# Second half of batch 0 as three one-pass products instead of four-pass ones, with a newly ordered step list

## The chip, the cores and the metric

The kernel runs on one core of one Trainium2 chip. The metric is the device time of one execution in microseconds (us), lower is better. In the profile the engines are PE (matrix multiply), PEld (its weight loads, which overlap the multiplies), DVE (vector), ACT (scalar), POOL (GpSimd) and SP (which issues most of the transfers).

## What is computed

Two blocks follow each other. The first is a chunked linear scan with decay (4 batches, 8 heads, 768 positions, head size 32, state size 16). The second is a mixer on its output, laid out as 4 batches of 768 positions by 256 channels. The weights reach the kernel as 64-bit floats.

```python
for c in range(nc):                                  # the scan, chunk by chunk
    cum = np.cumsum(la, axis=-1)
    M = CB * L                                       # L = exp(cum_i - cum_j), causal
    y[:, :, sl] = einsum(M, xc) + einsum(Cc, state) * exp(cum)
    state = decay_full * state + sum(Bx)
...
h = xt @ U @ V                                       # the mixer, rank 32 over positions
u = x + h.transpose(0, 2, 1)
ch = np.maximum(u @ w_ch1, 0.0) @ w_ch2              # 256 -> 1024 -> 256 channels
return (u + ch)
```

## The kernel before

**The order is written out by hand.** The string `PLAN` is a list of words; `follow` takes them one after another, and each word calls one small function that issues its instructions to the queues of the engines. Each engine works through its own queue strictly in that order. Nothing is scheduled by a compiler, so the position of a word in the list decides what stands ahead of it on every engine that it uses. Two more strings, `BANKS` and `SLOTS`, hold one letter or digit for each allocation, in the order of the list: `BANKS` says which of the 8 banks of the accumulator memory a result goes to, `SLOTS` which of 15 buffers (a to o, tile `words`) a piece of weights or of hidden values takes.

**The scan.** A batch is 768 positions in three pairs of 128-position blocks, so there are twelve pairs, k = 0 to 11. For each of them the words `P T g m M s u i n j y t` scale, transpose, form the products and their causal mask, carry the state, and copy the result out (`yT`, and by `t` the transposed `ytok`). `B` and `X` load its inputs, `E` issues PE fillers that keep the array busy.

**The mixer of a batch b.** `p`, `q` and `a` make `u = x + h` in place in `yT`. Each batch is cut into two halves of 384 positions, j = 0 and 1. Then come the two large products, in one of two ways:

- *plain* (line 813, word `U b.j.m`): full 32-bit products, which the array does in four passes. For one of the 8 groups m of 128 hidden channels, two matmuls of 128x384 read `w1f` (the first weights) and `yT`; ACT writes `relu` into `gT`. The second product (word `d b.j.k.n`, line 845) then takes 4 pieces n of two four-pass matmuls of 128x256.
- *in three parts*: word `S` (line 795) splits `u` into a rounded part, a remainder and a combination; ACT makes the first, DVE the other two. Word `f` (line 821) issues 6 one-pass matmuls of 128x384; ACT writes the rounded `relu`, and word `h` (line 831) has DVE write the remainder, and for every odd m also the combination of a pair (`joined`). The second product then takes 6 pieces of four one-pass matmuls of 128x256. The results carry the factor 1/`MORE`, which `summed` and the scale of `pT` (line 752) take out again.

Before the change, batch 0 is done plainly in both halves (`PLAIN = 2`, and `parts = b or j >= PLAIN` in `down`), batches 1 to 3 in three parts. The last piece of each `d` adds one more matmul, the sum on DVE (`ytok`) and the store.

**The weights.** Words `w` load pieces of the 64-bit weights. Word `c` turns a piece into 32-bit floats in three steps: two DVE operations and one on ACT, then one on DVE, then one on POOL. Word `R` makes the three parts of a piece, in two steps for the first weights (`R0` to `R3`: ACT; then POOL, ACT and DVE) and three for the second (`R4` to `R7`, DVE only in the third). The first weights in plain form (`w1f`) lie in the same buffer as the split `u` (tag "u", one buffer, lines 241 and 798). So the first `S` of the kernel can't write before the last `U` and the last `R0` to `R3` have read.

In all of it DVE's calls go through one helper at line 180, so its rows all carry that line; PE's mixer products all carry line 805.

Of the kernel before, what the change touches and what calls it, by code (L numbers as in the profile page):

```python
# [12 lines left out]
UINT32 = mybir.dt.uint32  # L13
FP32R = mybir.dt.float32r
WCOLS = 512
PLAIN = 2
BANKS = (
    '0120020340056712340512304672360475123605473605127463207546132076547654762054726013725472543176'
    '0176430253025301725301725164512513047640726134526130574062642026420135720457204132204620137374'
    '105743741065247346531057215231523175412376270376065262141645')  # L20
SLOTS = (
    'abcdefghijklmnocabidfejcgahfimjohimdfjohmlbkeongaecnifmknidjkbolhgacenjfidkmolbhcfgajkendgcloj'
    'amihbegadonfkmlbcf')


NEAR = 1.0 - 2.0 ** -13
# [1 line left out]
MORE = (1.0 + EPS) ** 2  # L28
LESS = 1.0 / (1.0 + EPS)
AF = mybir.ActivationFunctionType  # L30
ALU = mybir.AluOpType
# [7 lines left out]


PLAN = (
# [32 lines left out]


@with_exitstack
def kernel(
# [27 lines left out]
    nc = tc.nc  # L105
# [63 lines left out]
    class Kept:  # L169
# [15 lines left out]
    vector = Kept(nc.vector)  # L185
# [7 lines left out]
        out=a_sb,  # L193
# [46 lines left out]
    w1 = [const.tile([P, NCB, DF], FP32R, name=f"w1{i}") for i in range(3)]  # L240
# [487 lines left out]
    def mixer(b):  # L728
# [4 lines left out]
        def project():  # L733

            p = bank("w", DM)
            if b < 2:
                for c in range(NC):
                    nc.tensor.matmul(out=p[ts(c % 4, Q)], lhsT=U_sb[:, c], rhs=ytok[b][:, c],  # L738
                                     start=c < 4, stop=True, skip_group_check=True)
            else:  # L740
                seen = set()
                for c in range(0, NC, 2):
                    for half in range(NCB):
                        for v in range(2):
                            to = (c + 2 * half) % 4 + v
                            nc.tensor.matmul(out=p[ts(to, Q), ts(half, P)], lhsT=U_sb[:, c + v],  # L746
                                             rhs=ytok[b][:, c + v, ts(half, P)],
                                             start=to not in seen, stop=True, skip_group_check=True)
                            seen.add(to)
            hold["p"] = pT = mix.tile([P, DM], FP32, tag="pT", name="pT", bufs=1)  # L750
            if b:
                nc.scalar.activation(pT, p, AF.Copy, scale=1.0 / MORE)
            else:
                nc.scalar.copy(out=pT, in_=p)

        def parted():

# [18 lines left out]

        def summed(to, t, u):

            if b:
                return vector.scalar_tensor_tensor(out=to, in0=t, scalar=MORE, in1=u,  # L780
                                                   op0=ALU.mult, op1=ALU.add)
            return vector.tensor_tensor(out=to, in0=t, in1=u, op=ALU.add)

        def halves(near, far, both, v):

# [27 lines left out]
        def plain(j, m):  # L813

            if (j, m // 2) not in gT:
                gT[j, m // 2] = pair(FP32)
            t = bank("xz"[m % 2], HS)
            products(t, [(w1f[m // 2][:, n, ts(m % 2, P)], block(n, j)) for n in range(NCB)], True)
            nc.scalar.activation(gT[j, m // 2][:, m % 2], t, AF.Relu)

        def up(j, m):

# [165 lines left out]
```

## Time and profile before

| | us |
|---|---|
| time, median of 3 runs (lowest, highest) | 225.58 (222.82, 225.99) |
| time of the profiled execution | 226.02 |
| its span, first to last instruction | 224.3 |
| PE busy | 214.9 (96%) |
| DVE busy | 144.9 (65%) |
| ACT busy | 86.7 (39%) |
| POOL busy | 35.3 (16%) |

Busy time is an average over stages that differ. The first stage, up to about 36 us, is the scan of batch 0 with the first transfers; from there to about 70 us the plain products of batch 0 run beside the conversion of the weights and the scan of batch 1; the rest is batches 1 to 3. A row of the profile names the tile that is written, the tile read, the shapes, the count, the busy time and the mean of one in ns.

### The profile page before, as it was taken

The page shows a single profiled execution, that of the slowest core. Times are in us where ns is not written, and L with a number is a line of the kernel's source. Part 1 is how long each engine was busy: PE and PEld are TensorE (multiplying, and loading weights), DVE is VectorE, ACT ScalarE, POOL GpSimd, SP SyncE. Part 2 cuts the span into 40 slices and gives each one's busy share as a digit, 9 for nine tenths or more (in the row PEclk, how much of TensorE's full clock was granted, in tenths as well). Part 3 has the DMA queues.
Part 4 walks back from the last instruction along what each step waited for, and adds up shares of the span by engine and source line. Part 5 has one row for each costly group of instructions (what it writes and reads, how often), then busy time and mean ns, then how long its engine had stood idle before and what let it go on. Part 6 is the DMA issues. An engine that isn't in the chain of part 4 may idle for free.

```text
span 224.3 us, 6923 instructions
## 1 busy us (share of the span) xinstructions
PE 214.9 (96%) x3012; PEld 185.1 (83%) x3012; DVE 144.9 (65%) x300; ACT 86.7 (39%) x195; POOL 35.3 (16%) x49
## 2 busy tenths in 40 slices
PE   7888999999799999999999999999999999999994
PEld 4656655676466888998999999999999999999993
DVE  4697559587975882167693857757645955944651
ACT  2443742675486541143466022344623232232100
POOL 3012220526461390200000010200000000000000
PEclk9985799999999999999999999999999999999998
DMA  5988777888395500002144200100000000001012
GB/s 78 140 149 99 163 144 102 223 220 109 101 133 79 116 25 23 23 3 75 12 67 64 73 3 23 35 17 6 1 3 0 23 26 25 0 23 50 0 47 94
DMA packets 69662, 14.56 MB, mean 65 GB/s; under 512 B 63808, under 2 KB 67840, under 8 KB 69632
## 3 DMA queue, kind: packets, MB, share of 16 engines
q1 hardware_dynamic: 69488, 14.06, 32.1%
q8 instruction: 23, 0.38, 0.7%
q14 instruction: 7, 0.06, 0.1%
q10 hardware_dynamic: 144, 0.07, 0.1%
HBM read 10.98 MB, written 3.15 MB: 63 GB/s over the span
## 4 chain that ended last, share of the span: by engine, by line
PE 72%; DVE 2%; DVEq 0%; issue 0%
PE x L805 36%; PE z L805 25%; PE y L685 2%; PE w L712 2%; PE y L649 1%; PE x L535 1%; PE w L495 1%; DVE words L180 1%; PE w L569 1%; DVE w L180 1%; PE w L759 1%; PE w L746 1%; PE z L769 0%; PE x L769 0%; PE w L738 0%; PE z L535 0%
## 5 line engine op out<-in xcount | busy, mean ns | idle before, releaser
L180 DVE SCALAR_TENSOR_TENSOR words<-words 128x768 fp32r<-128x768 f32 (+3 forms) x35 | 29.3, 838 | 1.9 <-PE x L805 0.4
L805 PE MATMUL x<-w2c,words 128*128 128x256 f32 x160 | 30.1, 321 | 0.0
L805 PE MATMUL x<-u,w 128*128 128x384 f32 x144 | 29.9, 343 | 0.0
L805 PE MATMUL z<-u,w 128*128 128x384 f32 x144 | 29.2, 341 | 0.0
L805 PE MATMUL x<-w,words 128*128 128x256 f32 x192 | 29.1, 286 | 0.0
L829 ACT ACTIVATE words<-x 128x384 fp32r<-128x384 f32 x24 | 11.7, 491 | 37.8 <-PE x L805 37.7
L805 PEld LDWEIGHTS x<-w2c,words 128*128 128x128 f32 x160 | 24.9, 189 | 1.5
L805 PEld LDWEIGHTS x<-w,words 128*128 128x128 f32 x192 | 25.8, 190 | 0.1
L805 PEld LDWEIGHTS x<-u,w 128*128 128x128 f32 x144 | 24.6, 188 | 0.6 <-DVE u L180 0.3
L805 PEld LDWEIGHTS z<-u,w 128*128 128x128 f32 x144 | 24.8, 188 | 0.4 <-issue 0.2
L829 ACT ACTIVATE words<-z 128x384 fp32r<-128x384 f32 x24 | 11.8, 492 | 25.1 <-PE z L805 25.1
L180 DVE SCALAR_TENSOR_TENSOR words<-x,words 128x384 fp32r<-128x384 f32 x24 | 13.2, 552 | 10.6 <-ACT words L829 8.0
L180 DVE SCALAR_TENSOR_TENSOR words<-z,words 128x384 fp32r<-128x384 f32 x24 | 13.2, 550 | 5.8 <-ACT words L829 5.8
L180 DVE SCALAR_TENSOR_TENSOR S<-S,kept,w 128x64 f32<-128x64 f32 x40 | 11.2, 280 | 6.8 <-PE w L569 5.1
L805 PE MATMUL z<-w2c,words 128*128 128x256 f32 x80 | 15.3, 323 | 0.0
L685 PE MATMUL y<-M,x 64*32 64x64 f32 x768 | 13.1, 234 | 2.2 <-DVE M L180 1.8
L805 PE MATMUL z<-w,words 128*128 128x256 f32 x96 | 15.0, 285 | 0.0
L685 PEld LDWEIGHTS y<-M,x 64*32 64x32 f32 x768 | 9.2, 112 | 6.6 <-issue 2.5
L596 POOL TENSOR_TENSOR Sm<-S,own 128x256 f32<-128x256 f32 (+1 forms) x12 | 7.8, 650 | 36.1 <-DVE S L180 36.1
L805 PEld LDWEIGHTS z<-w,words 128*128 128x128 f32 x96 | 13.2, 189 | 0.1
L805 PEld LDWEIGHTS z<-w2c,words 128*128 128x128 f32 x80 | 12.5, 189 | 0.7
L535 PE MATMUL x<-Cm,T 32*64 32x128 f32 x192 | 11.4, 317 | 1.2 <-ACT Cm L505 0.7
(142 smaller groups left out, 356.1 us busy)
## 6 DMA issues: line engine op xcount, KB each, us to landing
words<-in_moe_w_ch_dram SPq DMA_DIRECT2D x7, 512.0 KB, 5.8
x<-in_x_dram SPq DMA_DIRECT2D x24, 128.0 KB, 3.4
out_dram<-ytok SPq DMA_DIRECT2D x23, 128.0 KB, 1.7
bc<-in_B_dram SPq DMA_DIRECT2D x24, 64.0 KB, 3.0
bc<-in_C_dram SPq DMA_DIRECT2D x12, 128.0 KB, 3.3
words<-in_moe_w_ch_dram SPq DMA_DIRECT2D x2, 256.0 KB, 5.1
words<-in_moe_U_dram SPq DMA_DIRECT2D x1, 192.0 KB, 3.2
words<-in_moe_V_dram SPq DMA_DIRECT2D x4, 48.0 KB, 2.1
```

The costliest lines, as they stand in the source:

```text
L180: self.last = call(*args, **kwargs)
L495: nc.tensor.transpose(out=tp[:, i, v], in_=s["BC"][:, i, c + v].rearrange("p h n -> p (h n)"), identity=ident)
L535: nc.tensor.matmul(out=s["g"][r][cols, c], lhsT=s["T"][rows, 0, c, cols], rhs=s["Cm"][rows, :, :, ts(2 * c + p, Q)].rearrange("r v t i -> ...
L569: nc.tensor.matmul(out=s["A"][p][ts(r, Q), v], lhsT=s["BC"][half, 0, v, 2 * r:2 * r + 2].rearrange("p h n -> p (h n)"), rhs=x_sb[k][half, ...
L596: nc.gpsimd.tensor_tensor(out=s["Sm"][:, sl], in0=s["S"][:, sl].rearrange("p i (s d) -> p i s d", s=2), in1=own2[:, b, 4 * q + sl.start:4 ...
L649: nc.tensor.matmul(out=channels(k)[r // 2][ts(r % 2, H), c, p], lhsT=own[ts(r, Q)], rhs=st[k]["T"][ts(r, Q), 1, :, ts(2 * c + p, Q)].rearr ...
L685: product = nc.tensor.matmul(out=y[n][ts(i, Q), c, p], lhsT=x_sb[k][half, c, h], rhs=s["M"][half, h // 2, c, h % 2], start=fresh(k, n, [i] ...
L712: nc.tensor.transpose(out=t[:, c, g], in_=yT[b][:, g, ts(2 * q + c, P)], identity=ident)
L746: nc.tensor.matmul(out=p[ts(to, Q), ts(half, P)], lhsT=U_sb[:, c + v], rhs=ytok[b][:, c + v, ts(half, P)], start=to not in seen, stop=True ...
L759: nc.tensor.matmul(out=p, lhsT=spot.rearrange("p q r -> p (q r)"), rhs=hold["p"], start=True, stop=True, skip_group_check=True)
L805: nc.tensor.matmul(out=t, lhsT=lhsT, rhs=rhs, start=start, stop=True, skip_group_check=True)
L829: nc.scalar.activation(gs[j, m // 2][0][:, m % 2], t, AF.Relu, scale=NEAR)
```

## The change

`PLAIN` becomes 1. Half j = 0 of batch 0 is still done plainly, half j = 1 in three parts. In the list the 8 words `U0.1.m` go; `S0.1`, 8 words `f0.1.m`, 8 words `h0.1.m` and two more pieces for each of the three `d0.1.k` come in. Since both halves of a batch share `pT`, `ps` and `u`, batch 0 now carries the factor 1/`MORE` throughout: the conditions on `b` go, and the plain `relu` is scaled by it too. The last `U` of the plain half and all of `R0` to `R3` now stand ahead of `S0.1`.

The list, the banks (248 to 249 letters) and the slots (112 to 120) are new throughout; the multiset of all other words is the same but for the fillers (`E1` three times before; `E2`, then `E1` three times). Quoted of the list is the stretch from the first up product to the second split of batch 1.

```diff
-PLAIN = 2
+PLAIN = 1
...
-    'E1 E1 A0 YB0 YB1 Q1.0 Q0.0 Q0.1 YX0 A1 Q0.2 Q1.2 K0 YB2 YU0 YV0 V0.0.0 E1 V0.1.1 V1.0.2 s0 YX1 '
...
-    'T4 c1 X5 w3 w4 g3 j2 c2 m3 c2 y2 T4 c2 M3 O2.1 p0 c1 g4 m4 q0 n3 M4 s3 a0.0 a0.1 c1 c3 U0.0.1 '
-    'U0.1.1 c3 U0.0.0 j3 c3 P5 s4 w5 u3 R0 R1 T5 U0.0.3 u4 T5 P6 U0.1.0 i3 g5 w7 y3 i4 M5 c4 n4 s5 '
-    'B10 X6 m5 c4 c5 c5 c4 U0.0.2 t3 T6 T6 U0.1.3 U0.1.2 B7 j4 n5 c6 y4 w6 c5 u5 g6 M6 i5 R1 R2 '
-    'U0.1.5 c6 c8 U0.0.6 m6 B9 c8 s6 j5 y5 n6 X7 U0.0.4 R3 U0.1.6 P7 T7 T7 R0 X8 c6 t5 t4 c7 c8 '
-    'U0.1.7 R3 U0.0.7 U0.0.5 c7 R2 B8 U0.1.4 p1 u6 w8 s7 X9 R4 j6 u7 g7 m7 i6 q1 P8 c7 c9 P10 '
...
+    'E2 YX0 A1 YB0 A0 Q0.0 Q0.2 YB1 Q0.1 K0 YX1 Q1.0 YB2 V0.0.0 YB3 YX2 V0.1.1 s0 E1 u0 g0 E1 B4 '
...
+    'y0 V2.1.3 n1 P3 g2 m2 P4 w1 s2 O0.0 M2 T3 T4 c0 u2 T3 i1 T4 j1 i2 c1 y1 g3 c1 n2 E1 j2 C0 y2 '
+    'C0 s3 m3 C0 t1 c0 c0 u3 w2 O2.1 v0 p0 M3 c4 c4 g4 c2 c2 q0 c2 n3 w4 c4 i3 m4 B5 a0.0 X4 c3 R2 '
+    'c3 a0.1 U0.0.1 c1 R2 R0 c3 R1 M4 X5 B6 U0.0.4 U0.0.0 U0.0.5 P5 c5 w6 U0.0.3 T5 T5 s4 j3 c5 R0 '
+    'y3 B8 c5 U0.0.2 u4 g5 R3 w5 i4 M5 X6 U0.0.6 B7 m5 n4 P6 n5 s5 R1 R3 w8 u5 c7 U0.0.7 j4 j5 S0.1 '
+    'c7 i5 y4 y5 T6 T6 P8 t3 c7 t4 t5 c6 c6 f0.1.2 f0.1.0 p1 c6 g6 h0.1.2 h0.1.0 R4 w7 M6 m6 s6 u6 '
+    'P7 f0.1.6 d0.0.0.0 f0.1.4 X8 R4 f0.1.3 c9 B11 d0.0.2.0 h0.1.6 c8 f0.1.1 q1 d0.0.1.0 d0.0.0.1 '
+    'c8 c9 d0.0.1.1 c8 h0.1.4 h0.1.3 d0.0.2.1 f0.1.7 c9 B9 R6 a1.0 d0.0.1.2 R5 h0.1.7 f0.1.5 R7 '
+    'd0.0.2.2 X7 d0.0.1.3 d0.1.2.0 R5 a1.1 d0.1.1.0 S1.0 d0.1.1.1 R6 T7 T7 d0.0.2.3 R7 P9 d0.0.0.2 '
+    'R4 T8 d0.1.2.1 d0.1.0.0 R5 f1.0.2 h0.1.1 R6 d0.1.0.1 h0.1.5 f1.0.4 d0.0.0.3 f1.0.5 d0.1.2.2 '
+    'B10 f1.0.6 d0.1.0.2 T8 d0.1.2.3 d0.1.0.3 h1.0.4 h1.0.2 R7 d0.1.1.2 h1.0.6 d0.1.2.4 d0.1.0.4 n6 '
+    'h1.0.5 s7 u7 f1.0.0 d0.1.2.5 d0.1.1.3 h1.0.0 d0.1.0.5 g7 i6 m7 j6 s8 f1.0.3 u8 y6 M7 d0.1.1.4 '
+    'd0.1.1.5 g8 h1.0.3 X9 i8 f1.0.7 f1.0.1 m8 M8 n8 X11 n7 i7 j8 s9 h1.0.7 j7 S1.1 h1.0.1 y8 T9 y7 '
...
@@ project
-            if b:
-                nc.scalar.activation(pT, p, AF.Copy, scale=1.0 / MORE)
-            else:
-                nc.scalar.copy(out=pT, in_=p)
+            nc.scalar.activation(pT, p, AF.Copy, scale=1.0 / MORE)
@@ summed
-            if b:
-                return vector.scalar_tensor_tensor(out=to, in0=t, scalar=MORE, in1=u,
-                                                   op0=ALU.mult, op1=ALU.add)
-            return vector.tensor_tensor(out=to, in0=t, in1=u, op=ALU.add)
+            return vector.scalar_tensor_tensor(out=to, in0=t, scalar=MORE, in1=u,
+                                               op0=ALU.mult, op1=ALU.add)
@@ plain
-            nc.scalar.activation(gT[j, m // 2][:, m % 2], t, AF.Relu)
+            nc.scalar.activation(gT[j, m // 2][:, m % 2], t, AF.Relu, scale=1.0 / MORE)
```

More of the change, by code (lines that the diff above doesn't have):

```diff
@@ L15 @@
 WCOLS = 512
-PLAIN = 2
+PLAIN = 1
 BANKS = (
-    '0120020340056712340512304672360475123605473605127463207546132076547654762054726013725472543176'
-    '0176430253025301725301725164512513047640726134526130574062642026420135720457204132204620137374'
-    '105743741065247346531057215231523175412376270376065262141645')
+    '0120203456700123445670142536742536017535607135442716047213560472013202135602136504726513715304'
+    '2671532041567320315310210167547645045301454130762541302764512643026423034104321506415730673241'
+    '0673410614564250164015735713713742746346101250615602734032473')
 SLOTS = (
-    'abcdefghijklmnocabidfejcgahfimjohimdfjohmlbkeongaecnifmknidjkbolhgacenjfidkmolbhcfgajkendgcloj'
-    'amihbegadonfkmlbcf')
+    'abcdefghijklmnofadichbemgkjodhbfmgimlhamegmengkmebjkcfdoclighmaonebckjfgldiombhekfacjgndileokm'
+    'ajghfbcodinlmekhancfgbjldi')
 NEAR = 1.0 - 2.0 ** -13
```

46 rows, old and new, of the table PLAN are left out of this document.

## The prediction

> **What bounds the kernel now.** I read the page first, then engine use by stretches, then PE's waits, the chain of waits, and the mean of each group of DVE instructions.
>
> ```profile
> span 224.3 us, 6923 instructions
> ```
>
> The profiled execution took 226.02 us: this span and 1.7 us around it. It lies 0.4 above the median of the three runs, 225.58, so 0.4 comes off any sum made against it.
>
> ```profile
> 10.00:15.00 5.00, 3.77 (x103) 2.18 (x103) 3.85 (x15) 2.54 (x10) 0.79 (x2) 0.98 0.87 152
> 15.00:25.00 10.00, 9.44 (x281) 6.58 (x281) 6.55 (x22) 4.82 (x16) 1.47 (x4) 0.50 0.87 137
> 36.00:70.00 34.00, 32.23 (x525) 20.89 (x528) 26.85 (x52) 21.26 (x47) 15.21 (x13) 1.00 0.72 142
> 55.00:60.00 5.00, 3.47 (x75) 2.00 (x75) 4.75 (x7) 3.27 (x7) 2.88 (x3) 1.00 0.35 112
> 70.00:221.00 151.00, 151.00 (x1790) 143.32 (x1782) 93.93 (x171) 49.65 (x104) 12.49 (x14) 1.00 0.13 32
> ```
>
> Columns: stretch, its length, then the busy time of PE, PEld, DVE, ACT and POOL, the granted clock, the DMA share and GB/s. From 70 us to the end PE never rests: what is taken from PE there comes off the time. From 36 to 70 us PE rests 1.8 us in 34, DVE is busy 79%. At 55 to 60 us the two change places: PE is at 3.47 of 5, DVE at 4.75. Before 25 us PE runs ten microseconds at half clock.
>
> The DVE timeline shows what made PE rest at 58 to 60 us, and the waits of PE name it:
>
> ```profile
> 57.61 1.84 DVE L180 TENSOR_SCALAR words<-words 128x512 f32<-128x512 f32 x2
> 59.37 0.74 DVE L180 TENSOR_TENSOR M<-x,causal 128x256 int32<-128x256 int32 x2
> ```
>
> ```profile
> PE y L685 <- DVE M L180: 1.5, 1, 1.5
> ```
>
> The opening of a `c` (two operations, 1.84) stood ahead of a mask, and PE waited 1.5 us for the mask. So batch 0 lives off two engines: its plain products need nothing of DVE, and DVE uses that time to prepare weights and scan. The change takes work from PE and puts work on DVE exactly there.
>
> **The change part by part.** PE first. The chain of waits gives what a piece takes where PE runs without a gap:
>
> ```profile
> 64.70 3.87 PE z L805 x12
> ...
> 73.44 1.73 PE x L805 x8
> ...
> 168.45 0.47 PE z L805 x4
> 168.93 1.05 PE x L805 x6
> ```
>
> A four-pass matmul leaves two records. The first row is three `U` (six matmuls): 1.29 us each. The second is two four-pass pieces of `d`: 0.865 each. The third is one piece of `d` in one-pass form, 0.47, and the last one `f`, 1.05. Eight `U` become eight `f`: 8 x (1.29 - 1.05) = 1.9 us less. Twelve pieces of `d0.1` become eighteen: 12 x 0.865 - 18 x 0.47 = 1.9 us less. PE loses 3.8 us of work, all of it later than the first up product.
>
> DVE's means, costliest first:
>
> ```profile
> L180 DVE SCALAR_TENSOR_TENSOR words<-words 128x768 fp32r<-128x768 f32 x24 | 23.0, 959 | 1.8 <-PE x L805 0.4
> L180 DVE SCALAR_TENSOR_TENSOR words<-z,words 128x384 fp32r<-128x384 f32 x24 | 13.2, 550 | 5.8 <-ACT words L829 5.8
> ...
> L180 DVE SCALAR_TENSOR_TENSOR S<-S,kept,w 128x64 f32<-128x64 f32 x40 | 11.2, 280 | 6.8 <-PE w L569 5.1
> L180 DVE TENSOR_TENSOR M<-x,causal 128x256 int32<-128x256 int32 x24 | 9.0, 418 | 5.1 <-PE z L535 5.0
> ...
> L180 DVE SCALAR_TENSOR_TENSOR u<-yT,u 128x768 fp32r<-128x768 f32 x6 | 6.8, 1130 | 0.0
> L180 DVE TENSOR_TENSOR u<-yT,u 128x768 fp32r<-128x768 f32 x6 | 6.6, 1107 | 2.8 <-ACT u L800 2.8
> L180 DVE TENSOR_TENSOR BC<-bc,F 128x512 f32<-128x512 f32 x9 | 6.3, 697 | 0.0
> L180 DVE TENSOR_SCALAR words<-words 128x512 int32<-128x512 int32 x7 | 6.2, 889 | 0.0
> L180 DVE SCALAR_TENSOR_TENSOR w<-words,w 128x512 fp32r<-128x512 f32 x4 | 5.9, 1486 | 1.4 <-POOL words L452 1.4
> L180 DVE SCALAR_TENSOR_TENSOR words<-words 128x512 int32<-128x512 int32 x7 | 4.8, 683 | 0.1
> L180 DVE SCALAR_TENSOR_TENSOR ytok<-x,ytok 128x256 f32<-128x256 f32 x11 | 4.7, 424 | 9.2 <-PE x L805 9.1
> L180 DVE SCALAR_TENSOR_TENSOR yT<-x,yT 128x384 f32<-128x384 f32 x6 | 3.3, 554 | 2.7 <-PE x L769 2.6
> ...
> L180 DVE TENSOR_SCALAR words<-words 128x512 f32<-128x512 f32 x7 | 2.9, 419 | 0.0
> L180 DVE TENSOR_TENSOR words<-w,w 128x512 f32<-128x512 f32 x4 | 2.7, 684 | 0.0
> ```
>
> DVE gains `S0.1` (1.11 + 1.13), eight `h` at 0.55 and four joins at 0.96: 2.24 + 4.4 + 3.84 = 10.5 us. ACT gains the first part of the split:
>
> ```profile
> L800 ACT ACTIVATE u<-yT 128x768 fp32r<-128x768 f32 x6 | 5.0, 841 | 3.5 <-DVE yT L180 3.5
> ```
>
> It is 0.84 us on an engine with 13 us free between 36 and 70 us; nothing. The new factor costs nothing: the sums change their form, not their size (the row `ytok`, 0.42, is that form already), and ACT scales in the pass that it makes anyway.
>
> How fast does DVE work such a list off? Two of its rows mark the ends of a run in the present list, the last sum of `a0.1` and the last state step of `u6`:
>
> ```profile
> 36.91 0.55 DVE L180 TENSOR_TENSOR yT<-z,yT 128x384 f32<-128x384 f32 x1
> ...
> 68.08 0.92 DVE L180 SCALAR_TENSOR_TENSOR S<-S,kept,w 128x64 f32<-128x64 f32 x3
> ```
>
> Between 37.5 and 69.0, 31.5 us, the list has six openings of `c` (0.42 + 0.89), six second steps (0.68), three `P` (0.70), four masks of two (0.84), 15 state steps (0.28) and four `R` (1.49): 7.9 + 4.1 + 2.1 + 3.4 + 4.2 + 6.0 = 27.7 us by the means. That is 0.88 of list work in each microsecond, with some of the rest waits for PE.
>
> First cut in the new list, from the first up product to `f0.1.2`. DVE up to the end of the split: four `R`, three masks, two `P`, two openings and one second step of `c`, seven state steps, the split: 6.0 + 2.5 + 1.4 + 2.6 + 0.7 + 2.0 + 2.2 = 17.4 us. PE has eight `U` (10.3) and 15 steps of the scan. Their price comes from this row of the same stretch, line 805 alone (PE, PEld):
>
> ```profile
> 36.00:70.00 34.00, 22.35 (x64) 11.52 (x64) 1.00 0.72 142
> ```
>
> 32.23 - 22.35 = 9.9 us for about 20 such steps of scan, 0.49 each (a pair of `T` as one); 15 make 7.4. PE: 17.7 us. At full pace DVE is ready, at 0.88 it needs 19.8 and PE waits 2.1. The chain at the split itself (`U0.0.7` must have read the buffer, then ACT 0.84, DVE 2.24: 3.1 us) lies under seven scan steps, `j4` to `t5`, 3.4 us; without them it would cost 3.1 in full. I take 1.0 for this wait, half way.
>
> Second cut, from the split on to `S1.1`, which `f1.1.7` needs. DVE: three openings and four second steps of `c`, three `P`, 15 `h` and seven joins, six masks, 11 state steps, the four sums of `a1`, six of `d0`, four last steps of `R`, two splits: 3.9 + 2.7 + 2.1 + 15.0 + 5.0 + 3.1 + 2.2 + 2.5 + 2.7 + 4.5 = 43.7 us. PE: 16 `f` (16.8), twelve four-pass pieces (10.4), 20 one-pass pieces (9.4) and 21 scan steps (10.3): 46.9 us before `p1`, `q1` and `a1` are counted. Over both cuts it is DVE 61.1 against PE 64.6: the first cut decides as long as DVE holds more than 0.92, and at 0.88 (69.4) the wait grows to 4.8.
>
> Ahead of the first up product DVE gets two more steps of `c4`, one of `c3` and `u3`, and loses `M4`: about 2.0 + 0.7 + 1.1 - 0.8 = 3.0 us more, against one more scan step on PE (0.5). Its cover is DVE's idle time there, 3.45 us from 15 to 25 us and 1.15 from 10 to 15. So 0 to 2.5; I take 0.7, nearer the covered end. The third filler `E1` stands where PE waits anyway.
>
> SP's queue: `X0` now goes out ahead of `B0`, by this row 1.6 us of issue:
>
> ```profile
> 5.43 1.57 SPq L208 DMA_DIRECT2D x<-in_x_dram  x2
> ```
>
> The first scaling may start later by up to 1.6, and `s0`, which needs `X0`, earlier by as much; I take 0. `w3` moves ahead of `w1` and all of the first weights come sooner; the DMA share is 0.72 to 0.87 there, so they fit.
>
> Sum against 226.0: PE -3.8; the old wait for the mask goes with the order that made it, -1.5 (0 if a like one comes instead); the wait at the split +1.0 (0 to 4.8); the start +0.7 (0 to 2.5). That gives 222.4; less 0.4 for the median, about 222.
>
> **The rivals.** *The half clock goes.* PE is at half clock from 15 to 25 us, and two of the new fillers stand just before. At full clock the stretch's PE work would take 4.7 us; DVE needs 6.55, so at most 3.45 is gained: 219 and, with no wait at the split, 217. For it: one run of three of the same kernel took 222.82, 3.2 less than the profiled one. Against it: nothing says that a filler of a few tenths decides. The longest wait that PE itself shows from 8 to 36 us is this:
>
> ```profile
> PE x L535 <- ACT Cm L505: 0.7, 1, 0.7
> ```
>
> [...]
>
> *DVE becomes the bound (slower).* Place: from the first up product to `S1.1`. If DVE works its 61.1 us of list off at 0.79 of the time, which is its busy share from 36 to 70 us, it needs 77.3 and PE waits 12.7 in all: 226.0 - 3.8 + 12.7 = 234.9, or 234.5 on the median. The point from which it shows as slower by 2% is a wait of 8.3, a pace of 0.84. For it: `h` waits for ACT, which waits for PE, so DVE's list is now full of steps that can't be done ahead; and accumulator banks stay taken until `h` has read them. Against it: 0.88 was reached while DVE waited for PE.
>
> **How the numbers follow.** The forecast, most of the saving left, has 0.46; its own range is 220 (no wait) to 226.5 (4.8, old wait replaced). The clock going has 0.26, at 217 to 221. DVE as the bound has 0.28, at 228 to 235, of which 0.02 lies inside 2%. Two per cent, about what a measurement of this kernel can tell from no change, is 221.1 and 230.1. Faster: 0.26 and 0.07 of the forecast's low end, 0.33. Slower: 0.26. Within: 0.41. The range 217.5 to 232 leaves out the end of the clock case and the upper half of the slow one.
>
> **What would show it.** Rows for `f0.1` at 1.05 for six and `d0.1` at 0.47 for four; 56 thirds instead of 48 and 28 joins instead of 24. PE should show a wait on DVE's `u` of about 1 us near 56 us, and be dense from there. The half clock shows in the granted clock. If PE waits over 5 us for DVE's `words`, `u` or M between 55 and 105 us, DVE was the bound; if PE is dense from 40 us on, the forecast is too high.

## The result, and the profile after

| us | before | after |
|---|---|---|
| median (lowest, highest), 20 runs each, same chip | 225.20 (222.82, 227.25) | 222.36 (221.63, 224.09) |
| time of the profiled execution, its span | 226.02, 224.3 | 223.10, 221.4 |
| start of the first up product, in the profile | 36.21 | 37.44 |
| start of the last matmul, in the profile | 220.77 | 217.81 |
| the stretch between these two | 184.56 | 180.37 |

The ratio of the times is 0.9904, 95% interval [0.9876, 0.9932]. The stretch became 4.19 us shorter, and it began 1.23 us later: 2.96 us, as the spans say (2.9). All experiments below are read by these two marks, the first row of line 801 (805 before) and the last. Some runs of each kernel fall into a slower state, which the medians contain and the ratios leave out.

The page after, its busy times and the granted clock in 40 slices:

```profile
span 221.4 us, 7025 instructions
...
PE 210.0 (95%) x3054; PEld 186.6 (84%) x3054; DVE 151.7 (69%) x314; ACT 87.2 (39%) x196; POOL 35.8 (16%) x47
...
PEclk9995699999999999999999999999999999999999
...
PE 74%; DVE 10%; DMA 4%; SPq 4%; issue 2%; POOL 2%; ACT 2%; POOLq 0%; DVEq 0%
```

PE lost 4.9 us of busy time and DVE gained 6.8. The slices at 5 and 6 tenths show that the half clock has stayed. The last line is the chain that ended last; its shares can't be set beside those of before (PE 72%, DVE 2%), because that chain could be followed back only to 55 us. Its pieces say more: from 53.3 to 77.2 us it runs over DVE, ACT and POOL without a piece of PE, and from there nearly all of it is PE. So there is now a stretch in which DVE, not PE, carries the end:

```profile
71.52 2.04 DVE words L181
73.56 0.93 DVE yT L181 x2
...
74.99 1.85 DVE words L181
...
77.23 1.22 PE z L801 x8
```

The changed kernel in the stretches of the prediction (length, then PE, PEld, DVE, ACT, POOL, granted clock, DMA share, GB/s), and PE's waits from 36 us to the end:

```profile
15.00:25.00 10.00, 8.12 (x168) 5.52 (x168) 7.39 (x23) 4.10 (x11) 1.13 (x2) 0.56 0.85 150
...
36.00:70.00 34.00, 33.00 (x504) 24.89 (x504) 30.12 (x59) 21.58 (x47) 16.76 (x15) 1.00 0.78 149
55.00:60.00 5.00, 5.00 (x69) 4.15 (x68) 4.97 (x8) 4.70 (x11) 1.77 (x2) 1.00 0.86 129
70.00:218.00 148.00, 146.91 (x1828) 141.62 (x1826) 97.31 (x176) 49.08 (x103) 11.71 (x12) 1.00 0.14 32
```

```profile
PE y L686 <- POOL settled L609: 0.6, 1, 0.6
PE y L650 <- issue: 0.6, 1, 0.6
PE z L801 <- DVE ytok L181: 0.5, 1, 0.5
PE z L801 <- DVE yT L181: 0.4, 1, 0.4
```

The wait of 1.5 us for a mask is gone, and at 55 to 60 us PE is full where it was at 3.47 of 5. There is no wait for `u`: the split ended at 56.01 and `f0.1.2` began at 56.23, straight behind the transposes before it. In exchange PE, which was without a gap behind 70 us, now waits twice there: 0.5 us at 77.2 for a sum of DVE, 0.6 at 153.5 for POOL's `settled`. The third wait, "issue", is one for which the profile names nothing; the last section comes back to it.

What a product and a piece take on PE, where they follow each other (start, duration, line, operation):

```profile
81.74 1.22 PE L801 MATMUL x<-u,w 128*128 128x384 f32 x6
82.80 0.64 PE L801 MATMUL x<-w,words 128*128 128x256 f32 x4
83.27 1.04 PE L801 MATMUL x<-u,w 128*128 128x384 f32 x5
```

From start to start `f` takes 1.06 us and the one-pass piece of four matmuls 0.47, as taken. So a matmul called four-pass (1.29 for the two of a `U`, 0.865 for the two of a piece, two records each) took 3.6 to 3.7 times one called one-pass; that the array makes four passes for it isn't shown by any row, the word is only a name here.

DVE's groups by form, and its timeline where PE waits for the sum (a row with x2 holds two instructions):

```profile
L181 DVE SCALAR_TENSOR_TENSOR words<-words 128x768 fp32r<-128x768 f32 x28 | 28.8, 1029 | 3.7 <-PE z L801 1.3 <-PE x L801 0.7
...
L181 DVE TENSOR_TENSOR u<-yT,u 128x768 fp32r<-128x768 f32 x7 | 6.7, 953 | 0.8 <-ACT u L796 0.8
L181 DVE SCALAR_TENSOR_TENSOR u<-yT,u 128x768 fp32r<-128x768 f32 x7 | 6.7, 950 | 0.0
...
L181 DVE SCALAR_TENSOR_TENSOR w<-words,w 128x512 fp32r<-128x512 f32 x4 | 3.0, 779 | 0.0
```

```profile
70.82 0.55 DVE L181 SCALAR_TENSOR_TENSOR words<-z,words 128x384 fp32r<-128x384 f32 x1
71.52 2.04 DVE L181 SCALAR_TENSOR_TENSOR words<-words 128x768 fp32r<-128x768 f32 x1
...
74.99 1.85 DVE L181 SCALAR_TENSOR_TENSOR words<-words 128x768 fp32r<-128x768 f32 x1
76.76 0.41 DVE L181 SCALAR_TENSOR_TENSOR ytok<-z,ytok 128x256 f32<-128x256 f32 x1
```

POOL in the same stretch:

```profile
69.85 2.90 POOL L439 TENSOR_TENSOR w2c<-words 128x512 int32<-128x512 int32 x2 [4.12 <-DVE words L181]
73.50 4.48 POOL L453 TENSOR_TENSOR words<-w2c,w 128x512 f32<-128x512 f32 x3 [0.76 <-ACT w L449]
```

Two of the four new joins began while POOL was at work and took 2.04 and 1.85 us instead of 0.96. The first ended only 0.8 us after POOL's row, at 73.56; a third (0.55) beside the same POOL row was not slowed. In the same way four `R` steps that took 5.9 us before take 3.0 in the new list, and the two parts of a split 0.95 each, not 1.11 and 1.13. DVE's timeline of the kernel before has the `R` steps one by one:

```profile
61.24 1.77 DVE L180 SCALAR_TENSOR_TENSOR w<-words,w 128x512 fp32r<-128x512 f32 x1
64.88 1.75 DVE L180 SCALAR_TENSOR_TENSOR w<-words,w 128x512 fp32r<-128x512 f32 x1 [1.17 <-POOL words L452]
67.15 0.68 DVE L180 SCALAR_TENSOR_TENSOR w<-words,w 128x512 fp32r<-128x512 f32 x1
```

POOL worked there from 60.85 to 62.46 and from 63.35 to 66.08. The opening of `c`, whose two steps read one operand each, is slowed too. In the kernel before it took 0.75 us alone and 1.84 where POOL worked beside it, and that was the opening that the mask, and with it PE, had to wait for:

```profile
46.31 0.75 DVE L180 TENSOR_SCALAR words<-words 128x512 f32<-128x512 f32 x2
57.82 1.35 POOL L438 TENSOR_TENSOR w2c<-words 128x512 int32<-128x512 int32 x1 [1.28 <-DVE words L180]
```

So about 1.1 of PE's old wait of 1.5 us can be laid to POOL. What these steps cost in the two profiles depended on whether POOL was at work when they began: 0.96 against 1.85 and 2.04 for a join, 0.68 against 1.07 to 1.77 for an `R` step, 0.42 against up to 1.55 for a step of an opening.

### The profile page after: what moved, and what is told of

It reads as the page before. It is cut to its first block, busy times and chain, and to the rows that moved or that the text cites. A ratio compares the mean times of both kernels' runs of the same rounds, so it can differ in the third digit from the quotient of the medians.

```text
span 221.4 us, 7025 instructions
## 1 busy us (share of the span) xinstructions
PE 210.0 (95%) x3054; PEld 186.6 (84%) x3054; DVE 151.7 (69%) x314; ACT 87.2 (39%) x196; POOL 35.8 (16%) x47
## 4 chain that ended last, share of the span: by engine, by line
PE 74%; DVE 10%; DMA 4%; SPq 4%; issue 2%; POOL 2%; ACT 2%; POOLq 0%; DVEq 0%
PE x L801 34%; PE z L801 24%; DVE words L181 4%; SPq L209 4%; PE y L686 3%; PE y L650 3%; DMA bc<-in_C_dram 2%; PE w L496 2%; PE x L536 2%; DMA bc<-in_B_dram 2%; DVE S L181 1%; PE w L570 1%; DVE M L181 1%; PE w L713 1%; DVE yT L181 1%
## 5 line engine op out<-in xcount | busy, mean ns | idle before, releaser
L181 DVE SCALAR_TENSOR_TENSOR words<-words 128x768 fp32r<-128x768 f32 (+3 forms) x39 | 35.1, 903 | 4.0 <-PE z L801 1.3
L801 PE MATMUL z<-u,w 128*128 128x384 f32 x168 | 34.7, 343 | 0.0
L801 PE MATMUL x<-u,w 128*128 128x384 f32 x168 | 34.3, 342 | 0.0
L801 PE MATMUL x<-w,words 128*128 128x256 f32 x224 | 34.0, 285 | 0.0
L801 PEld LDWEIGHTS x<-w,words 128*128 128x128 f32 x224 | 30.5, 190 | 0.3
L801 PEld LDWEIGHTS z<-u,w 128*128 128x128 f32 x168 | 28.9, 188 | 0.5
L801 PEld LDWEIGHTS x<-u,w 128*128 128x128 f32 x168 | 28.7, 188 | 0.3
L801 PE MATMUL x<-w2c,words 128*128 128x256 f32 x144 | 25.5, 305 | 0.0
L181 DVE SCALAR_TENSOR_TENSOR ytok<-x,ytok 128x256 f32<-128x256 f32 (+1 forms) x17 | 6.7, 406 | 10.8 <-PE x L801 10.7
L181 DVE TENSOR_TENSOR BC<-bc,F 128x512 f32<-128x512 f32 (+2 forms) x18 | 10.0, 570 | 4.5 <-ACT F L391 2.1
```

The source lines that it names most:

```text
L181: self.last = call(*args, **kwargs)
L801: nc.tensor.matmul(out=t, lhsT=lhsT, rhs=rhs, start=start, stop=True, skip_group_check=True)
```

## The experiments

The theory: the two halves of PE's saving (U to `f`, one-pass pieces in `d0.1`) stay on the path, since PE remains the bound nearly everywhere; DVE just keeps up. Rivals: the gain is the order alone; it is the old wait alone; DVE is the bound from 56 us on. A row of the table is one profiled execution, and the ratio comes from the timed runs beside runs of the kernel before on the same chip. The chips differ from row to row (the kernel before took 224.65 to 225.68 us on those of the experiments), so rows are compared by the stretch and the ratio, not by the median:

| kernel | first up product | last matmul | between | median us | ratio to before [95%] |
|---|---|---|---|---|---|
| before | 36.21 | 220.77 | 184.56 | 225.20 | |
| after | 37.44 | 217.81 | 180.37 | 222.36 | 0.9904 [0.9876, 0.9932] |
| after_again | 39.03 | 219.39 | 180.36 | 223.03 | 0.9896 [0.9844, 0.9948] |
| e1_order_only | 36.91 | 223.48 | 186.57 | 228.66 | 1.0208 [1.0161, 1.0256] |
| e2_factor_only | 34.86 | 221.14 | 186.28 | 225.31 | 1.0031 [0.9992, 1.0069] |
| e3_joins_on_act | 36.55 | 216.23 | 179.68 | 221.84 | 0.9896 [0.9846, 0.9947] |
| e4_fewer_pieces | 36.66 | 214.93 | 178.27 | 220.52 | 0.9842 [0.9791, 0.9893] |
| e5_fillers | 37.35 | 219.62 | 182.27 | 225.23 | 1.0010 [0.9971, 1.0050] |
| e6_joins_twice | 36.44 | 220.78 | 184.34 | 229.04 | 1.0124 [1.0054, 1.0195] |
| e7_c8_behind_m6 | 34.22 | 217.53 | 183.31 | 223.08 | 0.9955 [0.9916, 0.9994] |
| e8_plain_twice | 33.91 | 227.21 | 193.30 | 232.58 | 1.0382 [1.0322, 1.0442] |
| e9_parts_twice | 38.72 | 230.50 | 191.78 | 233.65 | 1.0422 [1.0344, 1.0499] |
| e10_joins_later | 36.24 | 217.55 | 181.31 | 223.12 | 0.9939 [0.9906, 0.9972] |
| e11_two_moves | 37.05 | 216.78 | 179.73 | 222.25 | 0.9883 [0.9836, 0.9930] |

**The changed kernel once more.** For the spread of the two marks.

> The changed kernel itself, on the chip of the other three: 0.988 to 0.993 of the kernel before by the 20 runs that there are.

The start moved by 1.6 us and the stretch by 0.01. So differences of 0.5 us between stretches can be read where the waits and the clock agree; starts can't be compared from one profile each.

**The new list with the old arithmetic.**

```diff
-PLAIN = 1
+PLAIN = 2
...
-... j4 j5 S0.1 c7 ... f0.1.2 f0.1.0 p1 c6 g6 h0.1.2 h0.1.0 R4 ...
+... j4 j5 c7 ... U0.1.2 U0.1.0 p1 c6 g6 R4 ...
...
-... R4 T8 d0.1.2.1 d0.1.0.0 R5 f1.0.2 h0.1.1 R6 d0.1.0.1 h0.1.5 f1.0.4 ...
+... T8 d0.1.2.2 d0.1.2.3 d0.1.0.0 d0.1.0.1 f1.0.2 d0.1.0.2 d0.1.0.3 R4 R5 R6 f1.0.4 ...
```

> The new list with the old arithmetic: both halves of batch 0 plain, so the split, the thirds and two pieces of each second product of the half are gone, and three last steps of R stand some words later. By the theory (PE is the bound from the first up product on, so its 3.8 us less of work are the gain) the 3.8 us come back and DVE's 10.5 us go unnoticed: about 226, a ratio of 1.00 to the kernel before (0.995 to 1.01). By the rival that the gain is the new order it stays at 222.4, a ratio of 0.987 to 0.99.

It is 2.1% slower than before, more than the 1% that was allowed. The rival that the order brings the gain falls: without the one-pass products this order loses. Set against the changed kernel it is 1.0208/0.9904, 3.1% or 6.9 us, while the arithmetic takes 3.8 us from PE. The rest is the list, which was laid around the new products: three `R` steps had to move behind the `d0.1`, and PE stands at 18.84 of 20 us between 90 and 110. So this run separates the two parts only in sign. For DVE it separates them in size: with the same 300 steps as before, DVE is busy 141.1 us here, 3.8 less than the 144.9 of the old order, and the change adds 10.6 to that (151.7).

**The factor alone, in the kernel before** (the line in `summed` is changed too, as in the change itself)**.**

```diff
-            if b:
-                nc.scalar.activation(pT, p, AF.Copy, scale=1.0 / MORE)
-            else:
-                nc.scalar.copy(out=pT, in_=p)
+            nc.scalar.activation(pT, p, AF.Copy, scale=1.0 / MORE)
...
-            nc.scalar.activation(gT[j, m // 2][:, m % 2], t, AF.Relu)
+            nc.scalar.activation(gT[j, m // 2][:, m % 2], t, AF.Relu, scale=1.0 / MORE)
```

> The kernel before with its own list, but with the common factor in batch 0's sums, in pT and in the plain relu. The step on record says that it costs nothing: a ratio of 1.000 within 0.003. If the other form of the sum or the scale in relu cost even 0.05 us in each of the 28 places, it would be 1.4 us more, a ratio of 1.006.

1.0031 with 1 in the interval: no cost that was measured, though up to 0.7% isn't excluded by it. In the profile the stretch is 1.72 us longer than before, and that has another reason, which its windows around the old wait show:

```profile
57.00:58.60 1.60, 0.09 (x7) 0.04 (x3) 1.60 (x3) 0.65 (x2) 0.82 (x1) 1.00 0.00 0
...
61.00:62.00 1.00, 1.00 (x3) 0.62 (x2) 1.00 (x3) 0.62 (x2) 0.11 (x1) 0.50 1.24 152
62.00:63.00 1.00, 1.00 (x3) 0.39 (x3) 0.34 (x1) 0.39 (x1) 0.47 (x1) 0.50 0.76 117
63.00:64.00 1.00, 1.00 (x6) 0.64 (x5) 0.17 (x1) 0.22 (x1) 1.00 (x2) 0.74 1.20 192
64.00:66.00 2.00, 2.00 (x14) 1.60 (x13) 2.00 (x2) 2.00 (x6) 1.03 (x1) 1.00 0.71 111
```

PE rests 1.5 us at 57 to 58.6, and from 60 to 63.5 its clock is halved: some 3.4 us at half speed, 1.7 us lost. In the profile of the kernel before the same wait had no such sequel.

**The four joins of batch 0 on ACT.**

```diff
-                joined(*g)
+                if b:
+                    joined(*g)
+                else:
+                    nc.scalar.activation(g[2], g[1].bitcast(FP32), AF.Copy, scale=1.0 / EPS)
```

> The changed kernel, with the four joins of batch 0 moved from DVE to ACT as a scaled copy of the remainder (the subtraction of the rounded part is left out). DVE loses 3.8 us of work between 60 and 90 us, ACT gains about 3. By the theory (PE is the bound, DVE only just keeps up) the only wait that can go is the 0.5 us of PE before 77 us: 0 to 0.6 us less, ratio to the kernel before 0.985 to 0.991. By the rival that DVE is a second bound in this stretch it is 2 to 3.8 us less, ratio 0.973 to 0.982.

The stretch is 0.69 us shorter and the wait for the sum gone (from 70 to 90 us PE, first after the length, is full, DVE at 12.75):

```profile
70.00:90.00 20.00, 20.00 (x187) 19.17 (x189) 12.75 (x23) 14.43 (x27) 5.59 (x5) 1.00 0.37 60
```

Four joins less, some 5.8 us of DVE with the two that POOL held up, are worth 0.7 us, as the theory had it; in the timed ratio that doesn't show.

**The four joins twice.**

```diff
                 joined(*g)
+                if not b:
+                    joined(*g)
```

> The changed kernel with each of the four joins of batch 0 done twice on DVE: 3.8 us more of DVE between 70 and 90 us, where it is busy 18.2 of 20 us. If DVE only just keeps up, its 1.8 us of rest take the first part and PE waits for about 2: ratio to the kernel before 0.995 to 1.002. If DVE has room (later rest takes it all), under 0.5 us: 0.988 to 0.993. If DVE is a bound in its own right, all 3.8: 1.004 or more.

The stretch grows by 3.97 us, and PE waits where the theory had allowed it little:

```profile
70.00:90.00 20.00, 16.18 (x93) 14.25 (x92) 19.45 (x25) 9.44 (x18) 5.80 (x5) 1.00 0.23 40
```

```profile
PE z L802 <- DVE ytok L182: 2.7, 1, 2.7
PE x L802 <- DVE ytok L182: 0.6, 1, 0.6
```

The ratio is that of the rival, DVE as a bound in its own right. The four second joins are 4.9 us more on DVE, not 3.8, because here too POOL slows three of the eight (33.7 us for 32 joins, 28.8 for 28 after). Together: 4.9 us more on DVE cost 4.0, and taking 5.8 away gives 0.7. From 70 to 77 us the two engines are in balance: what is added to DVE is paid at about four fifths, what is taken away brings little.

**Six one-pass pieces less.**

```diff
-... d0.1.1.1 ... d0.1.2.2 B10 f1.0.6 d0.1.0.2 T8 d0.1.2.3 d0.1.0.3 ... d0.1.1.2 ... d0.1.1.3 ...
+... d0.1.1.1 ... B10 f1.0.6 T8 ...
```

> The changed kernel without the pieces 2 and 3 of the three second products of the half (the part with the remainders is left out): 24 one-pass matmuls, 24 x 0.118 = 2.8 us of PE's work. DVE, ACT and POOL have the same work. By the theory all of it comes off: about 219.5, a ratio to the kernel before of 0.975 to 0.98. If DVE is a second bound, less than 1 us comes off: 0.986 or more.

6 x 0.47 = 2.8 us less on PE made the stretch 2.1 us shorter, ratio 0.9842. That is neither the whole 2.8 of the theory nor the less than 1 of the rival: PE's work in `d0.1` is on the path at about three quarters of its price.

**Each first product of this half twice.** In the kernel before the plain ones, in the changed kernel the one-pass ones.

```diff
+            for again in range(1 + j):
                 products(t, [(w1f[m // 2][:, n, ts(m % 2, P)], block(n, j)) for n in range(NCB)], True)
```

> The kernel before, with the two matmuls of each of the eight words U0.1.m issued a second time with the same operands; nothing else is changed. It prices the plain first product of this half where it stands. If PE is the bound in that stretch and one U is worth 1.29 us, the profile's sum (first up product to the last second product, 184.4 us before) grows by 8 x 1.29 = 10.3 us, less what of PE's 1.8 us of rest from 36 to 70 us the extra work covers: +8.5 to +10.3, ratio 1.038 to 1.046. If a U costs 1.40 (22.35 us over 16 of them by the row of the stretch), it is +9.4 to +11.2, ratio 1.042 to 1.050. If DVE, not PE, sets the pace from 36 to 70 us, the second issue hides in part: under +7, ratio below 1.031.

```diff
+            for again in range(2 if (b, j) == (0, 1) else 1):
                 products(t, [(w1[v][:, n, ts(m, P)], us[j][v][:, n])
                              for v in range(3) for n in range(NCB)], True)
```

> The changed kernel, with the six matmuls of each of the eight words f0.1.m issued a second time with the same operands; nothing else is changed. By the theory that PE and DVE are in balance from 56 to 77 us and PE alone is the bound behind it, the eight second issues (8 x 1.05 = 8.4 us on PE) cost at least 7 and at most 8.4: first up product to last second product from 180.3 to 187.3 to 188.7, ratio to the kernel before 1.021 to 1.028. By the rival that DVE is the bound all through that stretch, PE's extra work hides under DVE's list and costs less than 4: ratio below 1.008. The difference to the run with the plain products doubled, 10.3 against 8.4, is the 1.9 us that the prediction put on the change from U to f.

The plain ones: +8.74 us. PE's rests from 36 to 70 us (1.8) are filled, and an "issue" wait of 1.1 is new, so eight `U` are worth 8.74 + 1.8 - 1.1 = 9.4 us, 1.18 each: nearer to 1.29 than to 1.40.

The one-pass ones: +11.4 where 7 to 8.4 was expected. The rival (DVE hides them) falls, and the theory misses by 3 us. The profile has them (windows; PE's wait):

```profile
114.00:116.20 2.20, 0.30 (x39) 0.19 (x20) 2.17 (x4) 0.42 (x2) 0.00 (x0) 1.00 0.34 49
116.20:118.00 1.80, 1.80 (x26) 1.71 (x26) 1.61 (x6) 1.40 (x5) 0.00 (x0) 0.84 0.04 9
118.00:120.00 2.00, 2.00 (x12) 2.00 (x11) 0.71 (x2) 1.64 (x4) 0.94 (x1) 0.50 0.00 0
120.00:122.00 2.00, 2.00 (x13) 1.97 (x13) 0.00 (x0) 0.40 (x1) 0.00 (x0) 0.79 0.00 0
```

```profile
PE y L686 <- issue: 1.9, 1, 1.9
```

At 114 us, 30 us behind the doubled products, PE waits 1.9 us for nothing that the profile names, and after it comes half clock again: 1.8 x 0.16 + 2 x 0.5 + 2 x 0.21 = 1.7 us. With 8.4 that makes 12.0, less the 0.5 of the vanished wait for the sum 11.5. The lowest of its six runs, 232.91, is 11.3 above the lowest after, so the timed runs carry something like it. What holds PE at 114 us is, as far as the last section can tell, its own instructions, of which this run has 96 more. So the pair doesn't price the step from U to `f`; the rows of the profile do.

**Fillers for the clock.**

```diff
-... s0 E1 u0 g0 E1 ... w3 V2.0.2 j0 y0 V2.1.3 ... T3 T4 ...
+... s0 E1 u0 F2 g0 E1 ... w3 F4 V2.0.2 j0 y0 F3 V2.1.3 ... T3 F1 T4 ...
```

> The changed kernel with ten more PE fillers (2.1 us of them at full clock) at four places between 9 and 23 us where PE waits, so that the clock may stay up in the start. By the rival on record a full clock from 15 to 25 us is worth up to 3.4 us: 219 to 220.5, a ratio to the kernel before of 0.975 to 0.98. By the theory that the start waits for DVE and its loads and not for PE (two experiments had the clock at 0.96 in that stretch by chance and began their first up product only 0.5 to 0.7 us sooner) it is at most 0.7 us, and the fillers may eat that: a ratio of 0.987 to 0.993.

The clock is whole in the profile, and nothing is won: the first up product starts at 37.35, and the time is that of before, above the 0.987 to 0.993 expected. Its windows and waits:

```profile
15.00:25.00 10.00, 7.87 (x214) 4.89 (x212) 6.07 (x20) 3.82 (x11) 0.66 (x2) 1.00 0.76 135
36.00:55.00 19.00, 16.70 (x278) 10.28 (x285) 14.14 (x31) 10.44 (x23) 10.38 (x10) 1.00 0.81 158
```

```profile
PE w L571 <- issue: 2.0, 1, 2.0
```

At full clock DVE does 6.07 us of work between 15 and 25, no more than at half clock (7.39), which fits a start that hangs on DVE and the transfers. But the run is no clean test of the clock: the fillers are PE work of their own, and PE has an "issue" wait of 0.8 us at 35 us, ahead of the first up product, that the changed kernel's profile doesn't have. The stretch is 1.90 us longer than after; 1.4 of that is the "issue" wait: 2.0 us at 51 us here, 0.6 at 48 us in the changed kernel. Whether it is in every run isn't known; the time as a whole, 1.001, says that the fillers cost about as much as the change had won.

**The old wait alone, in the kernel before:** the opening of `c8` behind the mask `m6` (two letters of `SLOTS` change places with it).

```diff
-    'U0.1.5 c6 c8 U0.0.6 m6 B9 c8 s6 ...
+    'U0.1.5 c6 U0.0.6 m6 c8 B9 c8 s6 ...
```

> The kernel before, with the opening of c8 moved behind m6 in the list, so that the two DVE operations that PE's one long wait was for (1.5 us at 58 to 60 us) no longer stand ahead of the mask. The step on record values that wait at 1.5 us: ratio 0.993. If another wait takes its place: 0.998 to 1.002.

PE is full from 55 to 70 us:

```profile
55.00:70.00 15.00, 15.00 (x271) 9.92 (x270) 13.15 (x24) 10.38 (x23) 7.63 (x7) 1.00 0.60 88
```

The stretch is 1.25 us shorter, the ratio 0.9955, between the two values named: about 1.0 us [0.1, 1.9] of the 2.2 us (0.96%) that the change brought. One word moved in the old list gives perhaps half as much as the whole change.

**Two joins later,** and then **two other moves,** both in the changed kernel with the same computation.

```diff
+                if (b, j) != (0, 1) or m not in (3, 7):
-                joined(*g)
+                    joined(*g)
...
-... d0.0.2.3 R7 P9 d0.0.0.2 ...
+... d0.0.2.3 R7 J0.1.3 P9 d0.0.0.2 J0.1.7 ...
```

> The changed kernel, with two of the four joins of batch 0 (those of f0.1.3 and f0.1.7, which took 2.04 and 1.85 us at 71.5 and 75.0 us beside POOL) issued later, behind the last steps of R7 and behind d0.0.0.2, where POOL rests; the same computation. By the theory that DVE and PE are in balance there and that the joins are slow only beside POOL, each join takes about 0.96 in its new place, PE's wait of 0.5 us for the sum at 77.2 us goes, and first up product to last second product falls from 180.3 by 0.3 to 0.8 us: ratio to the kernel before 0.986 to 0.989. By the rival that PE is bound by its own work there, nothing: 0.990. If a later reader of DVE's comes too late instead (the split of batch 1 or R5), 0.992 to 0.996.

The joins took 0.95 each in their new place, the wait for the sum went, and another came:

```profile
PE x L801 <- DVE words L181: 1.1, 1, 1.1
```

It stands at 83 us, where `f1.0` takes the accumulator bank that `h0.1.1` must have read; that `h` was now behind the two joins on DVE. Meanwhile DVE rested 2.44 us at 73 to 75 for PE. The stretch grew by 0.9.

```diff
-... f1.0.2 h0.1.1 R6 ...
+... f1.0.2 h0.1.1 J0.1.7 R6 ...
...
-... n11 d2.0.2.0 S2.1 j11 ... f2.1.0 d2.0.2.1 f2.1.2 ...
+... n11 d2.0.2.0 d2.0.2.1 S2.1 j11 ... f2.1.0 f2.1.2 ...
```

> The changed kernel, the same computation, with two moves: the join of f0.1.7 alone is issued later, behind h0.1.1 (so that it delays none of the steps that free a bank, as the two later joins did), and the piece d2.0.2.1 is taken ahead of the straight products j11, so that PE has another 0.47 us of work before the point where it waited 0.6 us for POOL's settled at 153.5 us. By the theory that these two waits, 0.5 and 0.6 us, are what the new list still leaves on PE behind 70 us, both shrink to 0.1 or less: PE 20.00 of 20 between 70 and 90 us, and first up product to last second product from 180.3 to 179.3 to 179.6, ratio to the kernel before 0.984 to 0.987. By the rival that a removed wait comes back at the next step that frees a bank, as it did with the two later joins, PE shows a new wait of 0.5 to 1 us on DVE's words between 75 and 95 us, the sum stays at 179.8 or more, and the ratio at 0.988 or more.

Both waits behind 70 us are gone from the profile, but for 0.3 at 84.6:

```profile
PE z L801 <- DVE words L181: 0.3, 1, 0.3
```

The stretch is 0.64 us shorter, less than the 0.8 to 1.1 expected, and the ratio 0.9883 can't be told from the change's 0.9904. It is the best full version by its middle value, faster than before, and not shown to be faster than after.

## Why the prediction was right

Predicted 222.0, measured 222.36 in the median; 222.4 against 223.1 for the profiled execution. The main term, PE's work less by 3.8 us and on the path, is right; its other terms are not all of the size that they were given. That the time came so near is in part luck: between the two profiles the wait at the split was 1.0 less than summed, the start 0.5 more, and new waits of 1.7 were not in the sum at all. The sum has a gain of 3.6, the two spans one of 2.9.

- *PE loses 3.8 us.* Right in kind, near in size. The rows after give 1.06 and 0.47; +8.74 us for eight more `U` and -2.1 for six pieces less show that these are on the path. The price of a `U` stays between 1.18 (e8), 1.29 (taken) and 1.40 (22.35 / 16, the row that the prediction itself shows for the stretch).
- *DVE gains 10.5 us.* Mis-sized: 6.8 of busy time. The work is there (28 joins, 56 thirds, 7 splits), and by e1 it adds 10.6; but the new order takes 3.8 off, which the prediction put at nothing. Its means came from an order in which POOL worked beside these steps: `R` 1.49 each against 0.78 after (2.8 us less for four), the parts of a split 1.12 against 0.95 (one split of six stood beside POOL). Two joins beside POOL went the other way (2.0 more). That the order does it and not the products is shown by e1: `R` at 0.776 and split parts at 0.953 there too.
- *The factor costs nothing.* Nothing measured (1.0031 [0.9992, 1.0069]).
- *A wait of 1.0 us at the split.* The step failed: 0. From the first up product to the end of the split DVE had 18.6 us, since PE itself took 18.8 (17.7 predicted), 0.6 of it the "issue" wait. With the prediction's count of 17.4 DVE worked at a pace of 0.94, not 0.88: it was ready as PE came. That the count comes near is luck: DVE was busy 16.7 of these 18.6 us with other parts, `R` 3.1 (6.0 counted), two `P` beside POOL 2.5 (1.4), the split 1.9 (2.2), and the rest of a `c3` and two sums of `a0.1`, which the list has ahead of the first up product.
- *The second cut hides behind the first.* In part wrong. DVE's list does run out of slack there, not at the split but at 70 to 77 us, by 0.5 us; e6 shows that it is a real bound (4.0 for 4.9 more).
- *The old wait, -1.5.* The profile's 1.5 is gone. By itself it is worth 1.25 in the stretch and about 1.0 in time. A new one of 0.6 at `settled` takes part of it back. The prediction laid it to the place of the opening alone; 1.1 of it came from POOL beside that opening.
- *The start, +0.7.* 1.23 in these two profiles. Over all with an unchanged first stage it is more: old list 36.21, 34.86, 34.22 and 33.91, mean 34.8; new list (all rows but the fillers) mean 37.2. That is 2.4, the far end of the 0 to 2.5. With it the sum is 2.4 - 4.19 = -1.8, where the ratio says -2.2 [-2.8, -1.5].
- *`X0` ahead of `B0`, `w3` earlier: 0.* Not tried by itself; it is in the start.

Against the profile of before the stretch has: -3.8 for PE, -1.5 for the mask, +0.6 +0.5 +0.6 of new waits, together -3.6; measured -4.19. The remaining 0.6 isn't assigned to anything.

The rivals. *The half clock goes:* in the profile it didn't (0.56 granted from 15 to 25 us). What it would be worth is not settled by the fillers, as said above. By chance the clock was whole in e8, and the old list began its first up product at 33.91 there; in the three other profiles of that list, with 10 to 14 us at half clock, it began at 34.22, 34.86 and 36.21. And the timed runs that the ratios count go with the clock: of the kernel before, 33 runs with a granted clock of 0.99 or more took 224.1 us in the median and 13 with 0.977 or less 225.4; of the changed kernel, 8 took 221.8 and 11 took 223.1. So the half clock goes with about 1.3 us in either kernel, less than the 3.45 at most; whether it causes them isn't shown. At like clock the change brings 2.2 to 2.3 us, so it isn't a gain of the clock. *DVE becomes the bound, 228 to 235:* it held PE for 0.5 us, not 8.3. The pace up to the split was 0.94, and the point given for it 0.84. But its place was well named: from 53 to 77 us the chain that ended last runs without PE, and e6 shows that what is added to DVE there is paid at four fifths.

Of the signs named, the products, pieces, counts and the half clock came as said; the wait for `u` didn't come, and PE wasn't dense behind it.

## What to carry to other kernels

Here a step's duration depended on its neighbours (0.96 us for a join alone, 2.04 for one beside POOL): before summing means from the old order, look which of them ran beside POOL, and price them alone and beside it. When work moves from a full engine to one with 20% idle time, count the second engine's list between two points where the first waits for it; where the two come out within a tenth, as here, an addition cost most of its price and a removal brought next to nothing. And before a large reordering, try the one word that ends the longest wait: here it gave perhaps half the gain.

## What the runs showed of the hardware

- Some DVE steps that began while POOL worked were held up until POOL's step had ended. Joins of 0.96 us alone took 2.04 and 1.85 beside it, and `R` steps of 0.68 alone took 1.75 to 1.77 in the kernel before; both have two operands in the main on-chip memory. The two slow joins ended 0.8 us, the three slow `R` 0.55 us after POOL's step did. Thirds, with one operand in an accumulator bank, kept 0.55. One step of an opening of `c`, with one operand, was held up as well: 0.42 alone, 1.49 to 1.55 six times in the profiles before and after, each ending 0.3 us after POOL's step. What makes DVE wait there isn't shown.
- A single rest of PE in a dense stretch was twice followed by half clock: 1.5 us of rest (e2) and 1.9 (e9), each followed, 1.3 to 1.5 us later, by about 3.4 us at 0.50, which costs 1.7 more. It wasn't always so: 1.5 in the kernel before, 2.0 in e5 and 2.7 in e6 had no such sequel. A wait on PE was thus sometimes worth twice its length. Why some rests had it and others not isn't shown.
- PE waits of 0.2 to 2.0 us whose cause the profile doesn't name ("issue") look in the traces like waits of PE for its own instructions. The page of the profile lists packets of instructions, in the changed kernel 24 on one queue, 0.39 MB or 16 KB each:

```profile
q8 instruction: 24, 0.39, 0.7%
```

  PE has 6165 recorded instructions there (multiplies, weight loads, semaphore steps), 257 for each packet. The fourteen profiles have 17 such waits. The one of the kernel before has 1217 of PE's recorded instructions ahead of it, the one of the changed kernel 1729, which is 512 or two blocks of 256 more; they ended 1.4 and 1.6 us after a packet had landed. Counted off from there in blocks of 256, no block of these two profiles begins sooner than 1.2 us after the packet of its number. In the second profile of the changed kernel, e4, e5, e9 and e10 nine such waits have about 601, 730, 854, 982 or 1876 matmuls ahead of them, steps of about 127, or 254 with the weight loads. This is read from the traces alone. So added instructions move these waits: the 0.6 at 48 us belongs to the new list (0.2 to 0.8 in nine of its ten profiles), and 1.1 in e8, 1.9 in e9 and 2.0 in e5 arose in runs that had added PE instructions. But 1.2 at 31 us in the second profile of the changed kernel is not in its first: such waits, 0.2 to 2.0 us long, limit what one profile can resolve.
